# Two banks for the tail's products, and the state added to its update on TensorE

## The chip, the cores and the metric

The kernel runs on one core of one Trainium2 chip. The metric is the device time of one execution in microseconds (us). Three runs of the kernel before took 725.43, 725.92 and 728.48 us, so the time before is the median, 725.92 us.

The core has five engines with a queue each: TensorE (PE, whose weight loads the profile lists as PEld), VectorE (DVE), ScalarE (ACT), GpSimd (POOL) and SyncE (SP), which here only issues DMAs. An engine works through its own queue in order. TensorE reads operands from the SBUF memory and writes results into PSUM, which has eight banks of 2 KB per partition; VectorE and ScalarE take the results out.

## The reference

Two computations in a row. The first is a linear recurrence for each of 4 x 8 batch-heads, over 768 time steps, with a 40 x 40 state:

```
for t in range(S):
    y[t]  = r[t] @ state
    Sa    = state @ a[t]
    state = state * w[t] - outer(Sa, b[t]) + outer(v[t], k[t])
```

The second, called mixture in the kernel, takes x, the y of all heads side by side (320 wide):

```
h = relu(x @ w_in);  u, v = h[..., :512], h[..., 512:]
v_n = (v - mean(v)) / sqrt(var(v) + 1e-6)
v_s = w_spatial @ v_n + b_spatial      # over the 768 positions
out = (u * v_s) @ w_out
```

## The kernel before

**Phase 1, the steps.** The recurrence is cut into chunks of 64 positions. One *step* takes one chunk of two batches, that is 16 batch-heads: four to a *group* g (0 or 1), in each of two *parities* (partitions 0 to 39 and 64 to 103). There are 24 steps: 0 to 11 for batches 0 and 1, 12 to 23 for batches 2 and 3. The state goes from step to step in the SBUF tile `Mc`; in steps 11 and 23 no state is handed on. For each step and group the chain is: `c_bp` (L535, products with the state), `c_bp_out` (L545), `c_ff` (L553), `c_ff_out` (L561), `c_xx` (L571, into a PSUM bank of the pool `ps_c`, shown as `ch`), `c_xx_out` (L582: two ScalarE copies that read that bank, then two GpSimd selects, L396), `c_mp` (L603: the state's update, written over the last 40 columns of the same bank), `c_mp_out` (L616 adds the old state, L617 multiplies by the decay `scn` and writes `Mc`), `c_y` (L627) and `c_y_out` (L640, which frees the bank that the next step's `c_bp` fills). Beside it run, for later chunks, the decays' scans and multiplications on VectorE (L281 to L313), a triangular inversion on VectorE (L345 to L362), and small products into the pool `ps_k` (shown as `bk`).

**The mixture's products.** For a block of 128 positions of two batches (12 blocks, j = 0 to 11) there are six products in the order u, u, v, u, u, v: `m_u` (L739, 8 matmuls of 256 columns, taken out by ScalarE at L741 and stored to DRAM as `uts`) and `m_v` (L694, 8 matmuls of 512 columns, taken out at L696, normalised, and stored as `vns`). That makes 72 products, k = 0 to 71. All write the one bank of the pool `ps_m` (tile name `pv`), so a product can start only when the one before has been taken out. Before a block's products, its inputs are loaded (`m_load`, one buffer) and split in two parts (`m_split`, two buffers). All products read the weights `wh`, `wl`.

**Phase 2.** For each batch b, `vload(b)` loads `vns` (L149) and `uts` (L158, into the tile `ut0` or `ut1`), `spatial` forms 18 matmuls (L173 to L175, tile `pg`) for each of 4 x 2 results, adds the bias (L177), multiplies by u (L178, needs `ut`) and splits; `proj` forms 12 matmuls for each of three results (L193, tile `po`). In the SBUF layout of the kernel before, `ut1`, the tile of batches 1 and 3, begins at byte 153,984 of a partition and is 12,288 long; `wh` begins at byte 156,128. So `ut1` can be loaded only when the last product has read `wh`.

**Order.** Phase 1's instructions stand in a plan with due times in steps, written by hand (`at(t, ...)`), and everything due before step 24 is issued in that order, on every engine. The products are due in slots, four to a step from step 11 on; 52 of the 72 (k = 0 to 51) are due before step 24. What is due later (the *tail*: products k = 52 to 71 with what belongs to them) is issued outside the part ordered by hand, together with phase 2. There the framework's planner sets each engine's order: earlier program text has precedence, but what its own model of the chip holds not to be ready (operand, buffer) is passed over, and later text fills the place. Phase 2's text stands behind the tail's.

**PSUM.** The pools hold, in the order in which they are opened: `ps_k` banks 0 and 1, `ps_c` 2 and 3, `ps_i` 4 (`itmp`, scratch of the inversion), `ps_b` 5 and 6, `ps_m` 7. Phase 2 uses banks 0 to 3 for `pg` and 4 to 6 for `po`.

Of the kernel before, what the change touches and what calls it, by code (L numbers as in the profile page):

```python
# [8 lines left out]
F32 = mybir.dt.float32  # L9
# [5 lines left out]
ALU = mybir.AluOpType  # L15
PSUM = bass.MemoryType.PSUM
DRAM = bass.MemoryType.DRAM

P = 128
C = 64  # L20
HB = 32
E = 40
NP = 4
NB = 2
# [7 lines left out]
DH = 512  # L32

@with_exitstack
def tile_kernel(ctx, tc, early, late, vtok, win, wspT, bsp, wout, out):
    nc = tc.nc
    dram = ctx.enter_context(tc.tile_pool(name="dram", bufs=1, space=DRAM))
    B = out.shape[0]
    S = out.shape[1]
    xs = dram.tile([B, 2, NP, E, S], F32, name="xs")  # L40
    vns = dram.tile([B, S // P, P, DH], F32, name="vns")
    uts = dram.tile([B // NB, S // P, DH // P, P, NB, P], F32, name="uts")
    with ExitStack() as c1:
        phase1(c1, tc, early, late, vtok, win, xs, vns, uts, dram)
    with ExitStack() as c2:
        phase2(c2, tc, vns, uts, wspT, bsp, wout, out)
# [165 lines left out]
def phase1(ctx, tc, early, late, vtok, win, xs, vns, uts, dscr):  # L212
    nc = tc.nc
    NS = early.shape[1]
    CPB = 12
    LO, HI = slice(0, 64), slice(64, 128)
    PR = (LO, HI)
    RR = (slice(0, E), slice(64, 64 + E))
    LV = slice(0, 64 + E)

    def pool(name, bufs=1, **kw):
        return ctx.enter_context(tc.tile_pool(name=name, bufs=bufs, **kw))
# [10 lines left out]
    moe = pool("moe")  # L233
    ps_k = pool("ps_k", 2, space=PSUM)
    ps_c = pool("ps_c", 2, space=PSUM)
    ps_i = pool("ps_i", 1, space=PSUM)
    ps_b = pool("ps_b", 1, space=PSUM)
    ps_m = pool("ps_m", 1, space=PSUM)

    warm = const.tile([P, 1], F32, name="warm")  # L240
# [10 lines left out]
    ident = const.tile([P, P], F32, name="ident")  # L251
    maskp = const.tile([P, C], F32, name="maskp")
    maskn = const.tile([P, C], F32, name="maskn")
    Mc = const.tile([P, NU, C], F32, name="Mc")
# [6 lines left out]
    st = {}  # L261
# [32 lines left out]
    def scr_store(s):  # L294
        if s % CPB == 0:
            return
        sv = st["raw", s][2]
        sc = jit.tile([P, NU], F32, name="sc")
        nc.scalar.activation(sc, sv[:, :, 1], AF.Copy)
        for par in range(2):  # L300
            nc.sync.dma_start(out=scr[s, par], in_=sc[RR[par]])
# [214 lines left out]
    def grp(g):  # L516
        return slice(g * NP, (g + 1) * NP), range(g * NP, (g + 1) * NP)

    def scn_load(s):
        if s % CPB == CPB - 1:  # L520
            return
        scn = jit.tile([P, E, NU], F32, name="scn", bufs=1)
        for par in range(2):
            nc.sync.dma_start(
                out=scn[PR[par]], in_=scr[s + 1:s + 2, par].broadcast_to([64, E, NU]),
            )
        st["scn"] = scn
# [67 lines left out]
    def c_mp(s, g):  # L595
        if s % CPB == CPB - 1:
            return
        gp, ns = grp(g)
        At, Rt, tk, xf = st["blk", s]
        mp = st["xx", g][:, :, C:]  # L600
        for q, n in enumerate(ns):
            for par in range(2):
                nc.tensor.matmul(  # L603
                    mp[RR[par], q, :], lhsT=Rt[par][:, n, C:], rhs=tk[:, n, par, :],
                    start=True, stop=True,
                )

    def c_mp_out(s, g):
        gp, ns = grp(g)
        if s % CPB == CPB - 1:  # L610
            if s < NS - 1:
                nc.vector.memset(Mc[:, gp, 0:E], 0.0)
            return
        mp = st["xx", g][:, :, C:]
        mn = jit.tile([P, NP, E], F32, name="mn")
        nc.vector.tensor_tensor(out=mn[LV], in0=mp[LV], in1=Mc[LV, gp, 0:E], op=ALU.add)  # L616
        nc.vector.tensor_tensor(  # L617
            out=Mc[LV, gp, 0:E], in0=mn[LV], in1=st["scn"][LV, :, gp].rearrange("p e n -> p n e"), op=ALU.mult
        )

    def c_y(s, g):
        gp, ns = grp(g)
# [9 lines left out]
    def c_y_out(s, g):  # L632
        gp, ns = grp(g)
        c = s % CPB
        Ev = st["pre", s][0].rearrange("p (n c) -> p n c", c=WSEG)
# [8 lines left out]
    def y_store(s, g):  # L644
        c = s % CPB
        if c % 2 == 0:
            return
        b = (s // CPB) * NB + g
        t0 = (c - 1) * C
        for par in range(2):  # L650
            nc.sync.dma_start(
                out=xs[b, par, :, :, t0:t0 + 2 * C].rearrange("n e t -> e n t"),
                in_=st["y", g][RR[par]],
            )
# [28 lines left out]
        split_lo(LO_ENG, xh[64:, 2], xt[64:, 2], xh[64:, 2])  # L683
        st["xhl", key] = (xh, xl)

    def m_v(g, bq, i):
        xh, xl = st["xhl", (bq, i)]
        pv = ps_m.tile([P, DH], F32, name="pv")
        vc = slice(DH, 2 * DH)
        mm = [(xh[:, k, g, :], wh[:, k, vc]) for k in range(3)]  # L690
        mm += [(xh[:, k, g, :], wl[:, k, vc]) for k in range(3)]
        mm += [(xl[:, k, g, :], wh[:, k, vc]) for k in range(2)]
        for j, (l, r) in enumerate(mm):
            nc.tensor.matmul(pv, lhsT=l, rhs=r, start=(j == 0), stop=(j == len(mm) - 1))  # L694
        vr = st["act"].tile([P, DH], F32, name="vr", bufs=2)
        nc.scalar.activation(vr, pv, AF.Relu)  # L696
        st["vr", g] = vr
# [30 lines left out]
        nc.scalar.activation(vr, vr, AF.Identity, bias=q[:, 2:3], scale=q[:, 1:2])  # L728
        nc.sync.dma_start(out=vns[bq * NB + g, i], in_=vr)

    def m_u(d, bq, i):
        xh, xl = st["xhl", (bq, i)]
        dc = slice(d * P, (d + 1) * P)
        pu = ps_m.tile([P, NB, P], F32, name="pv")
        mm = [(wh[:, k, dc], xh[:, k]) for k in range(3)]
        mm += [(wh[:, k, dc], xl[:, k]) for k in range(2)]
        mm += [(wl[:, k, dc], xh[:, k]) for k in range(3)]
        for j, (l, r) in enumerate(mm):
            nc.tensor.matmul(pu, lhsT=l, rhs=r, start=(j == 0), stop=(j == len(mm) - 1))  # L739
        ur = st["act"].tile([P, NB, P], F32, name="ur", bufs=2)  # L740
        nc.scalar.activation(ur, pu, AF.Relu)  # L741
        nc.sync.dma_start(out=uts[bq, i, d], in_=ur)
# [4 lines left out]
    def at(t, fn, *args):  # L747
        plan.append((t, len(plan), fn, args))
# [4 lines left out]
    v, p = nc.vector, nc.gpsimd  # L753
# [10 lines left out]
    for s in range(NS):  # L764
        at(s + 0.02, scn_load, s)
        for g in range(NB):
            at(s + 0.00 + 0.05 * g, c_bp, s, g)
            at(s + 0.04 + 0.05 * g, c_bp_out, s, g)
            at(s + 0.30 + 0.05 * g, c_ff, s, g)
            at(s + 0.34 + 0.05 * g, c_ff_out, s, g)  # L770
            at(s + 0.55 + 0.05 * g, c_xx, s, g)
            at(s + 0.60 + 0.05 * g, c_xx_out, s, g)
            at(s + 0.74 + 0.02 * g, c_mp, s, g)
            at(s + 0.755 + 0.02 * g, c_mp_out, s, g)
            at(s + 0.86 + 0.04 * g, c_y, s, g)
            at(s + 0.90 + 0.04 * g, c_y_out, s, g)
            at(s + 0.95 + 0.01 * g, y_store, s, g)
# [24 lines left out]
    for q in range(GS, NS):  # L802
        t = PREP.get(q, q - 8 + 0.01)
# [20 lines left out]
            at(T_DEC + i + k * 0.12 - (0.9 if k == 0 else 0), step, gen)  # L824
    at(T_DEC + 5.9, open_act)
    slots = [T_MOE + k // 4 + (M1, M2, M3, M4)[k % 4] for k in range(3 * NS)]
    for j in range(NS // 2):
        bq, i = j // 6, j % 6
        own = slots[6 * j:6 * j + 6]
        at(max(own[0] - 1.6, 2 * j + 2.1, T_DEC + 5.92), m_load, bq, i)  # L830
        at(max(own[0] - 0.7, 2 * j + 2.7), m_split, bq, i)
        for t, d in zip((own[0], own[1], own[3], own[4]), range(DH // P)):
            at(t, m_u, d, bq, i)
        for t, g in zip((own[2], own[5]), range(NB)):
            at(t, m_v, g, bq, i)
            at(t + 0.14, m_n1, g)
            at(t + 0.42, m_root, g)
            at(t + 0.48, m_n2, g)
            at(t + 0.76, m_n3, g, bq, i)
# [12 lines left out]
    with tc.manual_schedule():  # L852
# [6 lines left out]
        for q in range(P // HB):  # L859
            rows = slice(q * HB, (q + 1) * HB)  # L860
            p.affine_select(
                out=maskl[rows], in_=maskl[rows], pattern=[[1, HB]], base=0,
# [10 lines left out]
        for m, val in ((maskp, 1.0), (maskn, -1.0)):  # L873
            p.memset(m, val)
            for rows in PR:
                p.affine_select(
                    out=m[rows], in_=m[rows], pattern=[[1, C]], base=0,
# [51 lines left out]
        n = 0  # L929
        while plan[n][0] < NS:  # L930
            t, _, fn, args = plan[n]
# [59 lines left out]
```

## Time and profile before

| what | value |
|---|---|
| runs, median | 725.92 us (725.43 to 728.48) |
| the profiled execution's own time | 728.03 us |
| its span, first to last instruction | 726.2 us |
| mean granted TensorE clock | 0.901 of full |
| PE busy | 592.8 us, 82% |
| DVE busy | 448.6 us, 62% |
| ACT busy | 415.1 us, 57% |
| POOL busy | 289.7 us, 40% |
| step 0 starts (first L535) | 29.8 us |
| step 12 starts | 305.3 us |
| step 23 starts | 524.9 us |
| last product ends | 624.1 us |

How to read what follows: times are us from the first instruction. In a table of stretches each row is one stretch with its length, then each engine's busy time (and its instructions in brackets), then the granted clock of TensorE, the DMA engines' busy share and GB/s. In a row of groups, `x22 | 6.9, 315 | 7.5 <-PE ch L603 7.5` says 22 instructions, 6.9 us busy, 315 ns each, and 7.5 us in which the engine was idle just before them, ended by line 603's matmuls. In rows of the timeline the first number is the start, the second the time to the last one's end, and a bracket holds the idle time before and what ended it. A row of the chain of waits is start, length, and what the time went to; "issue" is time for which the profile shows no wait. An fp32 matmul of the program stands as two instructions in the profile.

### The profile page before, as it was taken

Reading aid. Unit: us, or ns where it says so; the run is one execution under the profiler, and the core shown is the slowest. Engines: PE = TensorE matmul, PEld = TensorE weight load, DVE = VectorE, ACT = ScalarE, POOL = GpSimd, SP = SyncE. Lnnn points to the kernel's source line nnn. Section 1 sums busy time; section 2 is a strip of 40 time slices with the busy share of each in tenths; the row PEclk is TensorE's granted clock in tenths of the full one; section 3 lists DMA queues with packets and bytes.
Section 4 is the critical chain, followed back from the end, with each engine's and each line's share of the span. In section 5 each row is a group of like instructions: output and inputs, shape, how many; then the busy total and the mean of one; then the engine's idle time right before and its main releaser. Section 6 shows DMA issues by size and latency. Waiting matters only on the chain. (4 is left out here: it accounts for less than half of the span.)

```text
span 726.2 us, 25447 instructions
## 1 busy us (share of the span) xinstructions
PE 592.8 (82%) x10784; PEld 535.0 (74%) x10784; DVE 448.6 (62%) x884; ACT 415.1 (57%) x904; POOL 289.7 (40%) x486
## 2 busy tenths in 40 slices
PE   2707776587776877989988999899999999599997
PEld 1606665586665776868877788788789998499997
DVE  7898689968999998758797565311247201343221
ACT  2406763377655666878878798798754423332112
POOL 4102230124433435354554543464549822373221
PEclk9956997578977888989999999999899999799999
DMA  9443675294444535454365344344263533650001
GB/s 186 86 90 69 104 145 112 51 185 94 106 91 101 112 82 118 112 126 112 102 187 165 85 133 127 106 120 116 73 198 108 158 108 100 189 180 34 28 28 55
DMA packets 101337, 81.35 MB, mean 112 GB/s; under 512 B 33576, under 2 KB 90152, under 8 KB 99304
## 3 DMA queue, kind: packets, MB, share of 16 engines
q1 hardware_dynamic: 100680, 78.01, 43.3%
q10 hardware_dynamic: 544, 1.72, 1.1%
q8 instruction: 85, 1.39, 0.9%
q14 instruction: 28, 0.23, 0.1%
HBM read 59.20 MB, written 20.50 MB: 110 GB/s over the span
## 5 line engine op out<-in xcount | busy, mean ns | idle before, releaser
L396 POOL TENSOR_SCALAR_AFFINE_SELECT Rt<-Rt 64x512 f32<-64x512 f32 (+1 forms) x144 | 84.1, 585 | 102.2 <-ACT Rt L582 74.4
L545 ACT ACTIVATE Rt<-bp 64x416 f32<-64x416 f32 x96 | 49.1, 512 | 68.2 <-PE bp L535 66.4
L351 DVE TENSOR_TENSOR itmp<-A 128x30 f32<-128x30 f32 (+9 forms) x180 | 73.7, 409 | 3.3
L396 POOL TENSOR_SCALAR_AFFINE_SELECT At<-At 64x512 f32<-64x512 f32 x48 | 36.9, 768 | 94.6 <-ACT At L406 92.5
L173 PE MATMUL pg<-wsh,vh 128*128 128x384 f32 x192 | 65.1, 339 | 0.0
L174 PE MATMUL pg<-wsl,vh 128*128 128x384 f32 x192 | 65.0, 339 | 0.0
L175 PE MATMUL pg<-wsh,vl 128*128 128x384 f32 x192 | 64.8, 337 | 0.0
L355 DVE TENSOR_TENSOR A<-A,itmp 128x30 f32<-128x30 f32 (+9 forms) x180 | 59.0, 328 | 6.2
L535 PE MATMUL bp<-lin,Mc 40*64 40x104 f32 x768 | 53.1, 301 | 11.1 <-DVE y L640 10.3
L535 PEld LDWEIGHTS bp<-lin,Mc 40*64 40x64 f32 x768 | 46.2, 167 | 16.0 <-DVE y L640 13.4
L177 DVE TENSOR_TENSOR g<-pg,bb 128x384 f32<-128x384 f32 x32 | 17.7, 553 | 63.9 <-PE pg L175 56.9
L702 DVE BATCH_NORM_STATS2 bs<-vr 128x6 f32<-128x512 f32 x24 | 16.6, 690 | 60.3 <-ACT vr L696 60.2
L54 POOL TENSOR_TENSOR gl<-g,gh 128x384 fp32r<-128x384 f32 x32 | 33.8, 1062 | 47.7 <-ACT gh L50 47.7
L582 ACT ACTIVATE Rt<-ch 64x416 f32<-64x416 f32 x96 | 49.2, 512 | 3.9 <-PE ch L571 1.5
L326 PE MATMUL bk<-at,sl 64*32 64x32 f32 x1536 | 24.4, 221 | 28.6 <-DVE sl L313 14.5
L553 PE MATMUL ch<-Rt,At 128*64 128x104 f32 x768 | 46.0, 277 | 1.2 <-issue 1.2
L50 ACT ACTIVATE gh<-g 128x384 fp32r<-128x384 f32 x32 | 16.7, 522 | 52.3 <-DVE g L178 52.3
L441 PE MATMUL bk<-ident,sl 128*128 128x128 f32 x192 | 31.7, 297 | 17.4 <-ACT tk L447 6.9
L553 PEld LDWEIGHTS ch<-Rt,At 128*64 128x64 f32 x768 | 40.3, 152 | 5.7 <-issue 3.0
L326 PEld LDWEIGHTS bk<-at,sl 64*32 64x32 f32 x1536 | 20.6, 132 | 30.7 <-DVE sl L313 14.6
L571 PE MATMUL ch<-ffs,xf 64*64 64x104 f32 x768 | 42.6, 263 | 0.0
L54 POOL TENSOR_TENSOR vl<-raw,vh 128x512 fp32r<-128x512 f32 x24 | 32.1, 1350 | 25.8 <-ACT vh L50 24.8
(121 smaller groups left out, 1604.2 us busy)
## 6 DMA issues: line engine op xcount, KB each, us to landing
ein<-in_early SPq DMA_DIRECT2D x40, 387.0 KB
lin<-in_late SPq DMA_DIRECT2D x48, 160.0 KB
uts<-ur SPq DMA_DIRECT2D x48, 128.0 KB
vns<-vr SPq DMA_DIRECT2D x24, 256.0 KB
raw<-vns SPq DMA_DIRECT2D x24, 256.0 KB
ut<-uts SPq DMA_DIRECT2D x24, 256.0 KB
Rt<-in_vtok SPq DMA_DIRECT2D x48, 80.0 KB
xs<-y SPq DMA_DIRECT2D x48, 80.0 KB
```

The lines of the kernel that those rows point to most:

```text
L54: eng.tensor_tensor(out=lo, in0=x, in1=hi.bitcast(F32), op=ALU.subtract)
L173: nc.tensor.matmul(pg, lhsT=vh[:, dc], rhs=w_h, start=(i == 0), stop=False)
L174: nc.tensor.matmul(pg, lhsT=vh[:, dc], rhs=w_l, start=False, stop=False)
L175: nc.tensor.matmul(pg, lhsT=vl[:, dc], rhs=w_h, start=False, stop=(i == NT - 1))
L326: nc.tensor.matmul(pl[o:o + HB, n, :], lhsT=sl[PR[par], n, par, cs], rhs=at[PR[par], n, cs], start=True, stop=True,)
L351: nc.vector.tensor_tensor(out=tp, in0=A[:, k + 1:, k:k + 1].broadcast_to([P, m, k]), in1=A[:, k:k + 1, 0:k].broadcast_to([P, m, k]), op=AL ...
L355: nc.vector.tensor_tensor(out=A[:, k + 1:, 0:k], in0=A[:, k + 1:, 0:k], in1=tp, op=ALU.add)
L396: nc.gpsimd.affine_select(out=t, in_=t, pattern=[[0, k], [1, C]], base=0, channel_multiplier=-1, compare_op=ALU.is_gt, fill=0.0,)
L535: nc.tensor.matmul(bp[PR[par], q, :], lhsT=Mc[RR[par], n, :], rhs=li[RR[par], n, C:], start=(q == 0), stop=False, skip_group_check=True,)
L545: nc.scalar.activation(Rt[par][PR[par], gp, :], st["bp", g][PR[par]], AF.Copy)
L553: nc.tensor.matmul(ff[PR[1 - par], q, :], lhsT=At[par][:, n, :], rhs=Rt[par][:, n, :], start=True, stop=True,)
L582: nc.scalar.activation(Rt[par][PR[par], gp], xx[PR[1 - par]], AF.Copy, scale=-1.0)
```

## The change

Three edits. First, `m_u` and `m_v` get a number k, and take the bank of `ps_i` instead of `ps_m` when it is odd. k is the product's slot number where the product is due at step 24 or later, and 0 otherwise; so products due in the tail alternate between two banks, and the others use `ps_m` as before. Second, the pool `ps_b` is opened ahead of `ps_i`: `ps_b` then lies in banks 4 and 5 and `ps_i` in bank 6. Third, in steps 0 to 11 (in effect 0 to 10, since step 11 hands no state on) `c_mp` first issues, for each group, eight matmuls of the identity with the old state into the place of the update, and the update's own matmuls add to them; the VectorE addition (L616) is left out in these steps, and the multiplication by the decay reads PSUM.

```diff
@@ phase1
+    ADD_PE = range(12)
...
+    ps_b = pool("ps_b", 1, space=PSUM)
     ps_i = pool("ps_i", 1, space=PSUM)
-    ps_b = pool("ps_b", 1, space=PSUM)
     ps_m = pool("ps_m", 1, space=PSUM)
@@ c_mp
+        add = s in ADD_PE
+        if add:
+            for q, n in enumerate(ns):
+                for par in range(2):
+                    nc.tensor.matmul(
+                        mp[RR[par], q, :], lhsT=ident[RR[par], RR[par]], rhs=Mc[RR[par], n, 0:E],
+                        start=(q == 0), stop=False, skip_group_check=True,
+                    )
         for q, n in enumerate(ns):
             for par in range(2):
                 nc.tensor.matmul(
                     mp[RR[par], q, :], lhsT=Rt[par][:, n, C:], rhs=tk[:, n, par, :],
-                    start=True, stop=True,
+                    start=not add, stop=True, skip_group_check=add,
                 )
@@ c_mp_out
+        sc = st["scn"][LV, :, gp].rearrange("p e n -> p n e")
+        if s in ADD_PE:
+            nc.vector.tensor_tensor(out=Mc[LV, gp, 0:E], in0=mp[LV], in1=sc, op=ALU.mult)
+            return
         mn = jit.tile([P, NP, E], F32, name="mn")
         nc.vector.tensor_tensor(out=mn[LV], in0=mp[LV], in1=Mc[LV, gp, 0:E], op=ALU.add)
...
+    def m_ps(k):
+        return ps_i.tile([P, DH], F32, name="itmp") if k % 2 else ps_m.tile([P, DH], F32, name="pv")
+
-    def m_v(g, bq, i):
+    def m_v(g, bq, i, k=0):
...
-        pv = ps_m.tile([P, DH], F32, name="pv")
+        pv = m_ps(k)
...
-    def m_u(d, bq, i):
+    def m_u(d, bq, i, k=0):
...
-        pu = ps_m.tile([P, NB, P], F32, name="pv")
+        pu = m_ps(k)[:, 0:NB * P].rearrange("p (g t) -> p g t", g=NB)
...
+    def tail(t):
+        return slots.index(t) if t >= NS else 0
+
...
-            at(t, m_u, d, bq, i)
+            at(t, m_u, d, bq, i, tail(t))
...
-            at(t, m_v, g, bq, i)
+            at(t, m_v, g, bq, i, tail(t))
```

More of the change, by code (lines that the diff above doesn't have):

```diff
@@ L614, in c_mp_out @@
         mp = st["xx", g][:, :, C:]
+        sc = st["scn"][LV, :, gp].rearrange("p e n -> p n e")
+        if s in ADD_PE:
+            nc.vector.tensor_tensor(out=Mc[LV, gp, 0:E], in0=mp[LV], in1=sc, op=ALU.mult)
+            return
         mn = jit.tile([P, NP, E], F32, name="mn")
         nc.vector.tensor_tensor(out=mn[LV], in0=mp[LV], in1=Mc[LV, gp, 0:E], op=ALU.add)
-        nc.vector.tensor_tensor(
-            out=Mc[LV, gp, 0:E], in0=mn[LV], in1=st["scn"][LV, :, gp].rearrange("p e n -> p n e"), op=ALU.mult
-        )
+        nc.vector.tensor_tensor(out=Mc[LV, gp, 0:E], in0=mn[LV], in1=sc, op=ALU.mult)
     def c_y(s, g):
```

## The prediction

> **What bounds the kernel now.** I read the page first, then busy time by stretch, then the chain of waits and the timeline at the places that these pointed to.
>
> Its rows of busy tenths show VectorE near full in the first third and TensorE in the last, so the change's two halves lie in stages with different limits. Two stretches of the steps (step 4; steps 5 to 9):
>
> ```profile
> core 0: us, PE busy (x) PEld busy (x) DVE busy (x) ACT busy (x) POOL busy (x), PEclk, DMA share, GB/s
> 143.88:165.29 21.41, 17.98 (x489) 16.20 (x489) 13.82 (x30) 13.42 (x29) 5.04 (x8) 0.74 0.79 162
> 165.29:266.37 101.08, 74.67 (x1962) 67.03 (x1961) 98.57 (x182) 65.26 (x145) 43.53 (x50) 0.82 0.45 99
> ```
>
> In steps 5 to 9 VectorE works 98.57 of 101.08 us and TensorE 74.67: what leaves VectorE there shortens the step. In step 4 VectorE works 13.82 of 21.41 us and TensorE 17.98; there the chain through TensorE sets the end.
>
> The tail, same columns: the last six products; the time to the next matmul; what follows; the rest.
>
> ```profile
> 609.68:624.10 14.42, 10.95 (x56) 8.05 (x55) 2.08 (x6) 4.54 (x10) 3.57 (x15) 1.00 0.27 89
> 624.10:631.28 7.18, 0.00 (x0) 0.00 (x1) 2.07 (x5) 2.19 (x5) 1.39 (x7) 0.69 0.95 262
> 631.28:637.10 5.82, 5.82 (x21) 5.82 (x22) 3.78 (x5) 1.99 (x4) 4.96 (x5) 0.50 0.59 191
> 637.10:722.10 85.00, 84.96 (x521) 84.70 (x519) 23.91 (x40) 21.09 (x44) 29.52 (x27) 1.00 0.19 62
> ```
>
> From 637 on TensorE never stops, so time that it loses before is lost at the end. It loses 3.47 us in the first row (14.42 less 10.95), 7.18 us in the second, and in the third it runs at half the clock: 5.82 us of work at 0.50 is 2.91 us lost. Sum: 13.56 us. The timeline and the chain of waits say why:
>
> ```profile
> 612.23 0.63 PE L739 MATMUL pv<-xh,wh 128*128 128x256 f32 x3 [0.69 <-ACT vr L696]
> ...
> 621.98 0.97 PE L694 MATMUL pv<-wh,xh 128*128 128x512 f32 x3 [0.52 <-ACT ur L741]
> 631.28 0.63 PE L193 MATMUL po<-woh,gh 128*128 128x320 f32 x1 [7.18 <-ACT gh L50]
> ```
>
> ```profile
> 623.73 0.37 SPq L158
> 625.31 4.72 DMA ut<-uts
> 630.11 0.57 DVE g L178
> ```
>
> Each of the last six products (first and last shown) waits 0.52 or 0.69 us until ScalarE has emptied the one bank. After the last, SP issues the loads of `ut1` (it lies on `wh`, which that product reads), VectorE waits for them at L178, and TensorE for the result. Before 609.68 other work covered such waits, and ran out:
>
> ```profile
> L173 PE MATMUL pg<-wsh,vh 128*128 128x384 f32 x84 | 28.5, 340 | 0.0
> L193 PE MATMUL po<-woh,gh 128*128 128x320 f32 x24 | 7.4, 309 | 0.0
> L739 PE MATMUL pv<-xh,wh 128*128 128x256 f32 x36 | 6.7, 294 | 0.4 <-ACT vr L696 0.4
> ```
>
> These groups are of 525.5 to 609.68. L173 to L175 take turns, so 3 x 84 = 252 matmuls of `spatial`: batch 0's 144, and 108 of batch 1, four results in PSUM and two in the buffers of g, where all of them wait for `ut1`. With 3 x 24 = 72 of `proj` that is all the filler there is. L739's idle time over twelve u products (3 of these matmuls each) is 0.4 us: while filler lasted, the one bank cost TensorE almost nothing.
>
> **Part 1, the tail's second bank.** No instruction is added. What changes is when a product may start, and so where the planner puts it. Before, it put some 22 fillers between two products; the real bank was free long before. The tail's first product, then a stretch further on:
>
> ```profile
> 545.77 0.61 PE L739 MATMUL pv<-xh,wh 128*128 128x256 f32 x3
> ...
> 561.54 0.28 PE L739 MATMUL pv<-xh,wh 128*128 128x256 f32 x1
> ...
> 562.75 0.39 ACT L741 ACTIVATE ur<-pv 128x256 f32<-128x256 f32 x1 [1.40 <-PE pv L739]
> ...
> 566.31 0.86 PE L694 MATMUL pv<-wh,xh 128*128 128x512 f32 x3
> ```
>
> The bank was empty at 563.14 and the next product began at 566.31: the planner had reckoned with a slower release. With two banks two products can follow each other, and only the third waits for a release. If the distance from a product's end to the next use of its bank stays 22 fillers, a pair takes about as much time as one product did: some 5 us (566.31 less 561.54, 4.8 us; each second pair's extra v product adds a microsecond). Twenty products from 545.77 then end near 545.8 + 10 x 5.3 = 599, not at 624. `ut1` needs the 7.18 us of before, so L178 can go on near 606, and the filler (the same work, TensorE never idle) lasts to 624.1 - 3.47 = 620.6. There is room of 14 us: even products that end at 613 would leave no hole. Then the waits, the hole and its slow clock all go: 13.56 us.
>
> Lower bound: the planner leaves the last six products behind the filler, and only the 3.47 us go (less than nothing only by late operands, a rival below). Upper: 13.56. I take 12.6, near the upper end, because the room is larger than the hole; the 1.0 us off is for two stalls like the 0.4 us above. What is late next: nothing in this stage but TensorE itself.
>
> The reordered pools cost nothing while `po` manages with two banks: its third is now the products' second, free only after the last odd product. A result takes 12 matmuls, 5.29 / 3 = 1.8 us, and is emptied in 434 ns, so two are enough; a wait there would hold `proj`'s next result alone.
>
> ```profile
> 658.16 5.29 PE po L193 x36
> L194 ACT ACTIVATE ot<-po 128x320 f32<-128x320 f32 x24 | 10.4, 434 | 18.9 <-PE po L193 18.8
> ```
>
> [...]
>
> **Part 2, the state added on TensorE.** Rows of L616 and L617 over 29 to 290 us (steps 0 to 10), then of L616 in steps 5 to 9; then four rows of step 7:
>
> ```profile
> L616 DVE TENSOR_TENSOR mn<-ch,Mc 104x160 f32<-104x160 f32 x22 | 6.9, 315 | 7.5 <-PE ch L603 7.5
> L617 DVE TENSOR_TENSOR Mc<-mn,scn 104x160 f32<-104x160 f32 x22 | 11.3, 511 | 0.8
> L616 DVE TENSOR_TENSOR mn<-ch,Mc 104x160 f32<-104x160 f32 x10 | 3.1, 311 | 0.0
> 218.65 0.51 PE L603 MATMUL ch<-tk,Rt 128*40 128x40 f32 x16 [0.49 <-ACT Rt L582]
> 223.27 1.08 PE L627 MATMUL bp<-Rt,tk 128*40 128x64 f32 x16
> 224.25 0.27 DVE L616 TENSOR_TENSOR mn<-ch,Mc 104x160 f32<-104x160 f32 x1
> 226.90 0.42 DVE L640 TENSOR_TENSOR y<-bp,Et 104x256 f32<-104x256 f32 x1
> ```
>
> Removed: 22 additions of 315 ns, 6.9 us or 0.63 us a step. Added: in each of 11 steps 2 groups x 8 fp32 matmuls, two instructions each, 32 with their weight loads. Their shape (40 x 40, 40 columns) is not in the trace; the nearest rows are
>
> ```profile
> 280.39 0.95 PE L603 MATMUL ch<-tk,Rt 128*40 128x40 f32 x32
> 279.31 1.15 PE L419 MATMUL bk<-lin 40*64 40x64 f32 x32
> ```
>
> Less the last one's 0.21 us, L603 takes one every 24 ns and L419 (40 rows too, 64 columns) 30 ns: 0.77 to 0.96 us a step, 8.4 to 10.6 us in all. I take 0.77, since 40 columns is L603's case. They wait for the same ScalarE copies (L582) as L603, since they overwrite what these read; the wait only moves ahead, and what is queued behind it on TensorE (L603, L627, the next step's L535) is late by 0.77 us.
>
> Where VectorE is the limit, that is covered: in step 7 L603 ends at 219.16 and L616 begins at 224.25; L627 ends at 224.35 and the last L640 begins at 226.90. In steps 2, 3 and 5 to 9 L616 never waits (idle 0.0 in 5 to 9; the 7.5 us of its waits lie in steps 0, 1 and 4), so 7 x 0.63 = 4.4 us are gained. In steps 0, 1, 4 and 10 VectorE waits for TensorE at L616 or L640: 0.77 more against 0.63 less, 4 x 0.14 = 0.6 us lost. Net 3.8 us; bounds: 6.9 if VectorE sets all eleven, and 8.4 us lost if TensorE does. Were VectorE's cover gone, a step would lose the 0.77 us.
>
> L617 then reads PSUM instead of SBUF. The nearest pair reads 384 columns, L177 from PSUM and L178 (its form's row) from SBUF:
>
> ```profile
> L177 DVE TENSOR_TENSOR g<-pg,bb 128x384 f32<-128x384 f32 x32 | 17.7, 553 | 63.9 <-PE pg L175 56.9 <-POOL gl L54 7.1
> L178 DVE TENSOR_TENSOR g<-g,ut x32: 544/558/1639, 547.4 to 712.2; 128x384 f32<-128x384 f32 x32
> ```
>
> 553 against a median of 558 ns: no charge. [...]
>
> **Sum.** 12.6 + 3.8 = 16.4 us off the profiled execution's 728.03 (span 726.2 and 1.8 around it) is 711.6. The median of the runs lies 2.1 us under that execution, so 709.5.
>
> **Rivals.**
>
> *The order of the tail stays* and only the six waits go, 3.5 us: 725.9 - 3.5 - 3.8 = 718.6. For it: the planner's reckoning isn't the chip's, and I infer its spacing. Against: the last block's split comes at 586.36 (below), and filler lasted 23 us longer.
>
> *TensorE sets the steps.* Part 2 loses up to 8.4 us instead of gaining; half of that, 4.2, with part 1 whole: 717.5. For it: step 4's row. Against: steps 5 to 9's.
>
> *Slower: products reach TensorE's queue ahead of their operands.* TensorE works in order, so a product placed earlier that waits for its split inputs or an eviction holds up all filler behind it. ScalarE, in order too, once stands still for 4.74 us behind a load, and the last block's split and a product's eviction stand behind it:
>
> ```profile
> 585.83 0.63 ACT L50 ACTIVATE vh<-raw 128x512 fp32r<-128x512 f32 x1 [4.74 <-DMA raw<-vns]
> 586.36 0.83 ACT L50 ACTIVATE xh<-xt 128x768 fp32r<-128x768 f32 x1
> 587.10 0.58 ACT L696 ACTIVATE vr<-pv 128x512 f32<-128x512 f32 x1
> ```
>
> If five of the tail's ten pairs met such a wait in full, 23.7 us against 16.4 gained, the time would be 725.9 + 7.3 = 733.2; it decides from 16.4 us of such stalls. Against: the tail's order had 0.4 us of them in 84, with this one in it.
>
> *It does not do what it says:* the planner uses the second bank but spaces products as before, the hole stays, and only part 2 counts: 722.1.
>
> **How the numbers follow.** Forecast 0.58 (709.5; its own range 705 to 714), tail's order stays 0.17, TensorE sets the steps 0.10, no effect in the tail 0.08, late operands 0.07. The range 703 to 720 reaches from all bounds at their best (725.9 - 13.6 - 6.9 = 705.4, and 2 us for the spread of runs) past the first two rivals. A change of 0.5% (3.6 us) is about what can be told from none: faster 0.83, same 0.10 (the fourth rival and a little of the second), slower 0.07.
>
> **What would show it.** Right: no idle TensorE over 1 us between 600 and 640, `ut1`'s loads issued some 15 us ahead of the filler's end, steps 5 to 9 shorter by 0.6 us each, L616 only from step 12. Wrong: a gap before a `po` matmul with a clock of 0.50 after it; L617 or L640 waiting for TensorE in steps 5 to 9; products idle on xh.

## The result, and the profile after

The changed kernel takes 707.31 us (705.49 to 711.40) against 725.67 (725.31 to 728.48): ratio 0.9728, 95% interval 0.9694 to 0.9763, 18.4 us less. A second series beside other kernels gave 706.63 against 725.97: ratio 0.9753 (0.9709 to 0.9797). Forecast were 709.5 us and a range of 703 to 720. The profiled execution is the slowest of its four: 711.40 us, span 709.5.

The tail first: busy time by stretch of the changed kernel, with the columns of the prediction's rows. The stretches are step 22, then 544.70 us to the end of the last product, and what follows up to 640 us:

```profile
503.00:522.81 19.81, 19.60 (x368) 16.49 (x368) 4.28 (x11) 16.71 (x38) 11.07 (x24) 1.00 0.33 96
...
544.70:598.63 53.93, 52.13 (x311) 48.97 (x310) 21.64 (x42) 24.88 (x51) 41.29 (x74) 1.00 0.48 145
598.63:640.00 41.37, 41.27 (x255) 40.95 (x254) 13.65 (x23) 14.37 (x32) 20.75 (x24) 1.00 0.57 179
```

Its timeline at the two waits that are left, at the last product, and at the loads of `ut1` and the first use of them:

```profile
583.42 0.63 PE L753 MATMUL pv<-xh,wh 128*128 128x256 f32 x3 [1.00 <-ACT ur L755]
...
586.12 0.62 PE L753 MATMUL itmp<-xh,wh 128*128 128x256 f32 x3 [0.78 <-ACT vr L710]
...
598.01 0.62 PE L708 MATMUL itmp<-wh,xl 128*128 128x512 f32 x2
601.30 5.38 SPq L158 DMA_DIRECT2D ut<-uts  x7
...
607.70 1.03 DVE L178 TENSOR_TENSOR g<-g,ut 128x384 f32<-128x384 f32 x2 [3.20 <-DMA ut<-uts]
```

The last product ends at 598.63 instead of 624.10, `ut1`'s loads are issued from 601.30 on, L178 goes on at 607.70, and TensorE works 41.27 of the 41.37 us from the last product to 640, at full clock. Neither the hole nor the half clock behind it is left. From the start of step 23 (the stretch of 201.25 us quoted below) the kernel takes 709.5 - 522.81 = 186.7 us, 14.6 less; step 22 takes 19.81 instead of 22.19, 2.4 less.

The steps. Steps 5 to 9 of the changed kernel, the same columns:

```profile
167.67:268.43 100.76, 79.89 (x2127) 71.86 (x2120) 96.35 (x175) 65.48 (x145) 43.97 (x50) 0.82 0.46 101
```

Groups of 29 to 290 us: the identity matmuls and the state's multiplication out of PSUM; then VectorE's waits in steps 5 to 9, where the kernel before had one, of 1.6 us at the row of L337:

```profile
L606 PE MATMUL ch<-Mc,ident 40*40 40x40 f32 x352 | 11.6, 210 | 4.0 <-issue 3.8
L626 DVE TENSOR_TENSOR Mc<-ch,scn 104x160 f32<-104x160 f32 x22 | 9.0, 435 | 10.8 <-PE ch L612 7.1 <-ACT Rt L430 2.8 <-ACT Rt L583 0.9
```

```profile
DVE Lc L338 <- PE bk L327: 1.3, 3, 0.6
DVE y L651 <- PE bp L638: 1.0, 1, 1.0
```

VectorE has 96.35 us of work in steps 5 to 9 instead of 98.57, and the steps take 100.76 instead of 101.08: in this execution the state's half bought next to nothing there. VectorE's wait for y (L651) is one of the signs that the prediction named for being wrong. So the gain lies where it was forecast, but the tail gave more than the bound of 13.56 us, and the state less than its 3.8. The experiments take these two apart.

### The profile page after: what moved, and what is told of

Its sections match the earlier page's. It is cut to its first block, busy times and chain, and to the rows that moved or that the text cites. A ratio compares the mean times of both kernels' runs of the same rounds, so it can differ in the third digit from the quotient of the medians.

```text
span 709.5 us, 26133 instructions
## 1 busy us (share of the span) xinstructions
PE 593.6 (84%) x11136; PEld 538.4 (76%) x11136; DVE 437.5 (62%) x862; ACT 414.7 (58%) x904; POOL 290.3 (41%) x486
## 5 line engine op out<-in xcount | busy, mean ns | idle before, releaser
L352 DVE TENSOR_TENSOR itmp<-A 128x30 f32<-128x30 f32 (+9 forms) x180 | 75.3, 419 | 3.2
L536 PE MATMUL bp<-lin,Mc 40*64 40x104 f32 x768 | 53.5, 302 | 15.4 <-DVE y L651 11.7
L536 PEld LDWEIGHTS bp<-lin,Mc 40*64 40x64 f32 x768 | 46.7, 168 | 18.3 <-DVE y L651 13.7
L554 PE MATMUL ch<-Rt,At 128*64 128x104 f32 x768 | 47.5, 283 | 0.0
L554 PEld LDWEIGHTS ch<-Rt,At 128*64 128x64 f32 x768 | 42.1, 158 | 4.5 <-issue 1.9
L716 DVE BATCH_NORM_STATS2 bs<-vr 128x6 f32<-128x512 f32 x24 | 16.6, 691 | 41.6 <-ACT vr L710 41.5
L638 PE MATMUL bp<-Rt,tk 128*40 128x64 f32 x768 | 32.5, 240 | 10.1 <-issue 10.1
L572 PEld LDWEIGHTS ch<-ffs,xf 64*64 64x64 f32 x768 | 38.3, 143 | 1.4 <-ACT Rt L583 0.2
```

The lines of the kernel that those rows point to most:

```text
L352: nc.vector.tensor_tensor(out=tp, in0=A[:, k + 1:, k:k + 1].broadcast_to([P, m, k]), in1=A[:, k:k + 1, 0:k].broadcast_to([P, m, k]), op=AL ...
L536: nc.tensor.matmul(bp[PR[par], q, :], lhsT=Mc[RR[par], n, :], rhs=li[RR[par], n, C:], start=(q == 0), stop=False, skip_group_check=True,)
L554: nc.tensor.matmul(ff[PR[1 - par], q, :], lhsT=At[par][:, n, :], rhs=Rt[par][:, n, :], start=True, stop=True,)
L572: nc.tensor.matmul(xx[ev, q, :], lhsT=xf[ev, n, :], rhs=ffs[ev, q, :], start=True, stop=True,)
```

## Experiments

Beside whole times, lengths of stages are used, since the early steps scatter from run to run (the last section has the stops behind it): one kernel measured twice (the wide identity, below) gave ratios of 0.9733 and 0.9826, while steps 14, 17, 18, 20 and 21 have the same length in every profile here to within some 0.1 us. A step runs from its first L535 matmul (L536 after the change) to the next step's. A *stop* is a time in which TensorE stands still in the middle of its work; for most stops of the early steps the profile shows nothing that TensorE waits for. A *pair* is one weight load and its matmul in the profile.

### Each half alone, and the whole again

Tail alone: 

```diff
-    ADD_PE = range(12)
+    ADD_PE = range(0)
```

> The second bank in the tail alone; the state is added on VectorE in all steps, as before. By the prediction part 1 is worth 12.6 us (bounds 3.5 and 13.56), so about 713 against 725.7, ratio 0.983. The profiled run of the changed kernel took 14.6 us less from step 23 on (186.7 against 201.25 us); if that is part 1 and the state part gives nothing, 711 and the same time as the changed kernel. If the state part is worth its predicted 3.8 us, this kernel is 3.8 us slower than the changed one; if the state part loses the 2.65 us by which step 12 began later in that profile, this one is 2.65 us faster.

Measured: 707.80 us, ratio 0.9758 (0.9713 to 0.9803). State alone:

```diff
     def tail(t):
-        return slots.index(t) if t >= NS else 0
+        return 0
```

(and `ps_i` ahead of `ps_b` again).

> The state added on TensorE in steps 0 to 11 alone; all products in one bank, PSUM pools in the old order. By the prediction -3.8 us: 721.9, ratio 0.995. By the profile of the changed kernel (step 12 began 2.65 us later than before): 725 to 728, ratio 1.000 to 1.004, with VectorE waiting for TensorE at the state's multiplication and at y. The rival that TensorE sets all steps: up to +8.4 us, 734.

Measured: 724.95 us, ratio 0.9987 (0.9950 to 1.0023). The whole again, on the same chip:

> The changed kernel again, beside the others on the same chip, in more rounds: 705.5 to 711.4, ratio 0.97 to 0.98. If places where TensorE stands still with nothing shown to wait for decide the step times, the start of step 12 moves by some 2 us from run to run; if the order of the work does, it stays within 0.5 us of the first profile's 307.99.

Measured: 706.63 us, ratio 0.9753 (0.9709 to 0.9797); step 12 began at 304.25, not at 307.99.

The tail alone is worth 18.2 us with an interval of 14.3 to 20.8; the state alone 1.0 us (3.6 less to 1.7 more); the whole is 1.2 us faster than the tail alone, which the scatter of the runs does not tell from nothing. The forecast of 12.6 lies below the tail's interval, that of 3.8 for the state just outside its own.

What the forecast of the tail missed is in step 22. The kernel before: the step in two parts, what follows it, then its timeline at the point between the parts:

```profile
502.76:517.85 15.09, 13.49 (x273) 11.87 (x273) 2.49 (x7) 13.91 (x32) 7.14 (x13) 0.99 0.32 88
517.85:524.95 7.10, 7.07 (x89) 5.47 (x89) 1.78 (x4) 3.21 (x8) 4.49 (x13) 0.54 0.27 80
524.95:726.20 201.25, 186.01 (x1184) 177.66 (x1184) 62.53 (x114) 64.49 (x134) 86.62 (x131) 0.97 0.34 107
```

```profile
516.28 0.51 PE L603 MATMUL ch<-tk,Rt 128*40 128x40 f32 x16 [0.40 <-ACT Rt L582]
517.85 0.77 PE L603 MATMUL ch<-tk,Rt 128*40 128x40 f32 x16 [1.07 <-ACT Rt L582]
```

And the kernel with the tail alone: step 22, what follows it, and its timeline at the same place:

```profile
501.44:521.25 19.81, 19.59 (x369) 16.50 (x369) 4.21 (x11) 16.71 (x38) 11.02 (x25) 1.00 0.33 96
521.25:707.60 186.35, 180.43 (x1176) 173.53 (x1176) 60.12 (x114) 64.17 (x135) 87.11 (x132) 1.00 0.37 116
```

```profile
512.71 0.63 PE L708 MATMUL itmp<-wh,xh 128*128 128x512 f32 x2
...
514.97 0.51 PE L612 MATMUL ch<-tk,Rt 128*40 128x40 f32 x16
515.40 0.50 PE L708 MATMUL itmp<-wh,xh 128*128 128x512 f32 x1
...
516.97 0.51 PE L612 MATMUL ch<-tk,Rt 128*40 128x40 f32 x16
```

The planner takes the first product of the second bank (k = 53, at 550.71 us in the kernel before) and puts it, in two pieces, just where TensorE stood waiting for ScalarE's copies (L582). Before, that stop took 1.07 us, and behind it TensorE ran at a mean clock of 0.54 to the step's end. What TensorE lost from step 22 on, before: 1.60 us idle and 7.07 x 0.46 = 3.25 us by the clock in step 22, then 0.45 + 3.47 + 7.18 idle, and 2.91 by the clock behind the hole, 18.9 us. After the change: 0.21 + 1.80 + 0.10 = 2.1 us idle up to 640, none by the clock. The difference, 16.8 us, is near what the whole stretch shows: 223.44 us before, 206.50 after, 16.9 less. The size depends on the execution. The kernel with the state alone has the same stop in step 22, followed by less time at half clock, and takes 21.18 us for that step and 224.37 from its start on; the second profile of the changed kernel takes 205.65 from there on, 18.7 less. The time won in step 22 appears partly behind it, since the product that fills the stop is no longer there.

### What of the second bank closes the hole

Two kernels with the state on VectorE. In one, only the very last product (number 71) uses the second bank; in the other, the first ten of the tail's twenty:

```diff
-        return slots.index(t) if t >= NS else 0
+        return slots.index(t) if slots.index(t) == 71 else 0
```

> Only the tail's very last product uses the second bank; state on VectorE. In TensorE's order 72 filler matmuls (some 23 us) then stand behind the last product and ahead of the first one that needs ut1, against none before and 117 in the changed kernel. Theory that the tail's gain is the hole: it closes although 19 of 20 products still share a bank; 7.18 us and the 2.91 us of half clock behind it go, most of the six waits for ScalarE and the stop in step 22 stay: -10.1 us, 716, ratio 0.986. Rival that every alternating product saves its share (17.3 us over 20 products): -0.9 us, 725.

```diff
-        return slots.index(t) if t >= NS else 0
+        return slots.index(t) if t >= NS and slots.index(t) < 62 else 0
```

> The tail's first ten products alternate, the last ten share one bank; state on VectorE. TensorE's order then has no filler between the last product and the first matmul that needs ut1, as before. Theory: the hole of some 7 us and its slow clock stay; what goes is the stop in step 22 (2.4 us in the profile of the kernel with the tail alone, by a product that fills it) and some 3 of the 3.47 us of waits: -5.4 us, 720.5, ratio 0.9926. Rival that every alternating product saves its share: -8.6 us, 717.

Measured: one product 721.88 us, ratio 0.9946 (0.9908 to 0.9984); ten products 720.32, ratio 0.9900 (0.9824 to 0.9975). By stage (step 22; the rest), the kernel with one product, with its waits from 504 to 640 us:

```profile
504.73:525.96 21.23, 19.29 (x360) 16.22 (x360) 4.11 (x11) 17.09 (x39) 11.61 (x25) 0.92 0.31 89
525.96:719.80 193.84, 183.74 (x1184) 175.25 (x1184) 61.13 (x114) 63.88 (x134) 86.96 (x131) 1.00 0.36 111
```

```profile
PE pv L708 <- ACT ur L755: 2.3, 2, 1.8
PE pv L753 <- ACT vr L710: 2.1, 3, 0.7
PE pv L753 <- ACT ur L755: 1.6, 3, 0.5
```

and the kernel with ten, with its timeline behind the last product:

```profile
502.27:522.07 19.80, 19.59 (x369) 16.50 (x369) 4.22 (x11) 16.70 (x38) 11.02 (x24) 1.00 0.34 96
522.07:718.90 196.83, 182.29 (x1176) 175.39 (x1176) 60.95 (x114) 65.04 (x135) 87.60 (x132) 0.98 0.35 110
```

```profile
616.58 5.18 SPq L158 DMA_DIRECT2D ut<-uts  x7
...
624.75 0.64 PE L193 MATMUL po<-woh,gh 128*128 128x320 f32 x1 [7.79 <-ACT gh L50]
```

One alternating product suffices to close the hole: no wait for `gh` is left, and step 23 on takes 7.4 us less. It is not the expected 10.1, because the waits for ScalarE rose to 6.0 us from 3.92 (0.45 + 3.47): eight products in a row now wait without filler instead of six. Ten alternating products fill the stop in step 22 (19.80 us again) and leave 2.6 us of waits for ScalarE out of 3.92, but the hole stays, 7.79 us long; from step 22 on this kernel takes 6.8 us less than before. So the two large terms belong to two different products, the first and the last. An equal share for each of twenty products (16.9 / 20) would have been 0.8 us for the one product, not 8.4. For the ten it would have been 8.5, which lies near the 6.8, but the hole that is still there speaks against it. In step 22 the two kernels are compared with a profile whose clock stayed low for long: the one-product kernel has the stop too, takes 21.23 us instead of 22.19, and so owes 1.0 of its 8.4 us to the clock and not to its product. The one-product kernel's whole time gained 3.9 us only by its ratio, less than its 8.4 from step 22 on; its profile reached step 22 2.0 us later than before, with the same order of work up to there, and the rest of that difference isn't explained.

### What the state's half costs and brings

First, one half exaggerated at a time. The identity matmuls issued three times:

```diff
-            for q, n in enumerate(ns):
-                for par in range(2):
+            for rep in range(3):
+                for q, n in enumerate(ns):
...
```

> As the changed kernel, with each step's identity matmuls issued three times into the same place (the first two are overwritten; same result): 1.54 us more TensorE work in each of 11 steps than in the changed kernel. If VectorE covers it, as predicted, in the seven steps 2, 3, 5 to 9, only the four others get longer: +6 us, 713. If TensorE sets all steps: +17 us, 724. If nothing but the stops without a shown wait count: 707.

Measured: 720.08 us, ratio 0.9926 (0.9888 to 0.9965). And the tail alone with VectorE's addition issued four times:

```diff
-        nc.vector.tensor_tensor(out=mn[LV], in0=mp[LV], in1=Mc[LV, gp, 0:E], op=ALU.add)
+        for rep in range(4 if s < 12 else 1):
+            nc.vector.tensor_tensor(out=mn[LV], in0=mp[LV], in1=Mc[LV, gp, 0:E], op=ALU.add)
```

> The second bank in the tail, the state added on VectorE and the addition issued four times in steps 0 to 10 (same result): 1.89 us more VectorE work in each of 11 steps than in the kernel with the tail alone (707.8). If VectorE sets seven steps, as predicted: +13.2 us, 721. If it sets all eleven: +20.8 us, 729. If TensorE sets them: 708 to 711.

Measured: 722.38 us, ratio 0.9987 (0.9954 to 1.0020). Steps 5 to 9 of the two, each in its own profile:

```profile
173.31:278.03 104.72, 83.27 (x2448) 75.50 (x2441) 96.46 (x175) 65.39 (x145) 43.38 (x50) 0.86 0.43 98
```

```profile
165.73:277.57 111.84, 75.17 (x1962) 67.56 (x1961) 108.30 (x212) 65.09 (x145) 44.79 (x50) 0.82 0.41 90
```

Without the state part these five steps take 101.20 us in the mean of five profiles (100.77 to 101.57), with it 99.53 in the mean of three (100.76, 99.27, 98.55). VectorE's 5 x 1.89 = 9.5 us more lengthened them by 10.6: VectorE does set these steps. But TensorE's 5 x 1.54 = 7.7 us more lengthened them by 5.2, where full cover would have been nothing. Of these 5.2 us step 8 has 2.9 (23.72 against 20.8): TensorE stood still within the update's products, with nothing shown to wait for, and VectorE waited for them:

```profile
252.96 0.63 PE L613 MATMUL ch<-tk,Rt 128*40 128x40 f32 x12 [3.46 <-issue]
253.73 0.43 DVE L627 TENSOR_TENSOR Mc<-ch,scn 104x160 f32<-104x160 f32 x1 [4.48 <-PE ch L613]
```

The whole kernels: with VectorE's addition fourfold 14.6 us more than the tail alone, where 13.2 were expected if VectorE sets seven steps; with the identities threefold some 13 us more than the changed kernel, between the expected 6 with cover and 17 without. Of these 13 us step 0 has 4.9 (46.88 us against 42.0 in the mean of three).

Then each part by itself. No addition on either engine in steps 0 to 10; the identity matmuls and VectorE's addition both (the matmuls' result is overwritten, `start=True` on the products); and 49 more identity matmuls in step 0 alone, for the place of instructions (the first and the third with `ADD_PE = range(0)`):

```diff
+        if s < 11:
+            nc.vector.tensor_tensor(out=Mc[LV, gp, 0:E], in0=mp[LV], in1=sc, op=ALU.mult)
+            return
         mn = jit.tile([P, NP, E], F32, name="mn")
```

> Second bank in the tail; in steps 0 to 10 the old state is neither added on VectorE nor on TensorE (that part of the computation is left out, the state is only the step's update times its decay). VectorE has 0.63 us a step less than in the kernel with the tail alone (707.8), TensorE's instructions are the same ones at the same places. If VectorE sets steps 5 to 9 down to that size, they take 101.2 - 3.2 = 98.0 us (101.2 is the mean of the four profiles without the state part) and the whole 4.4 us less, 703.4. If something else sets them as soon as VectorE has less, they stay above 100 and the whole within 1 us of 707.8.

```diff
-                    start=not add, stop=True, skip_group_check=add,
+                    start=True, stop=True, skip_group_check=add,
...
-        if s in ADD_PE:
-            nc.vector.tensor_tensor(out=Mc[LV, gp, 0:E], in0=mp[LV], in1=sc, op=ALU.mult)
-            return
```

> As the changed kernel with its identity matmuls, but their result is overwritten and the addition stays on VectorE (same result): TensorE's work and program of the changed kernel, VectorE's of before. If VectorE's addition is what counts in seven steps, as predicted: 4.4 us more than the changed kernel (711), 0.6 us more than the kernel with the tail alone. If TensorE's 0.77 us a step counts as well: up to 716. Steps 5 to 9 (99.5 us in the mean of three profiles with the state part, 101.2 without): 102.7 by the first, 101.2 or less if only the place of the stops counts.

```diff
+        if s == 0:
+            for rep in range(24 + g % 2):
+                nc.tensor.matmul(
+                    mp[RR[0], 0, :], lhsT=ident[RR[0], RR[0]], rhs=Mc[RR[0], ns[0], 0:E], start=True, stop=True,
+                )
```

> The kernel with the tail alone and 49 identity matmuls of 40 columns more in step 0, overwritten at once: 98 pairs of weight load and matmul, which puts every later TensorE instruction 98 pairs further on in its program, as the 352 pairs of the state part do from step 11 on if TensorE stops at every 127th pair (352 less 2 x 127 is 98). Theory that the stops without a shown wait belong to places in the program: steps 12, 13 and 15 take the lengths that they have with the state part (20.0, 20.3, 21.6 us in the mean of three profiles) and not those without it (23.3, 19.4, 20.6 in the mean of four). Rival that the state part itself shortens step 12: 23.3, 19.4, 20.6 stay. Time: 707.8 - 3.3 + 0.9 + 1.0 and some 2.4 us for the 49 matmuls in step 0, 709.

Measured: without any addition 705.69 us, 2.1 less than the tail alone, ratio 0.9712 (0.9658 to 0.9766); both 711.35, ratio 0.9799 (0.9756 to 0.9841); 49 more in step 0 713.87, ratio 0.9833 (0.9788 to 0.9878). Steps 5 to 9 without any addition, then with both:

```profile
165.89:263.30 97.41, 72.49 (x1961) 64.82 (x1960) 94.64 (x172) 65.38 (x145) 44.46 (x50) 0.87 0.46 102
```

```profile
170.35:272.57 102.22, 77.00 (x2129) 69.11 (x2121) 99.06 (x184) 65.39 (x145) 43.72 (x50) 0.85 0.45 98
```

These steps took the lengths that were expected if VectorE sets them (98.0 and 102.7); the whole without any addition lies between its two expectations, 703.4 and some 707.8, and the whole with both at its lower one, 711. The four corners of steps 5 to 9: VectorE's addition alone 101.20, neither 97.41, identities alone (the change) 99.53, both 102.22. Taking the addition away saves 3.8 us without the identities and 2.7 with them, 3.2 in the mean, and 5 x 0.63 = 3.15 was forecast. Putting the identities in costs 2.1 without the addition and 1.0 with it, where nothing was forecast. The change keeps 1.7 of the 3.2. Two of the corners are single profiles, and the three of the change differ by 2.2 us, so these costs are rough. VectorE's idle time in the five steps (their length less its busy time) is steadier: 2.5 to 2.8 us in the five profiles with the addition alone, 2.77 with neither, 4.41, 4.14 and 3.16 with the identities, 3.16 with both. By it the identities make VectorE wait 1.1 us more without the addition and 0.6 more with it, in the mean; what is left of the 2.1 and 1.0 is VectorE's own work between the marks, which also scatters (95.13 to 96.35 us in the three profiles of the change).

The third kernel tests where steps change length. Step 12 of the kernel before, of the changed kernel, and of the one with 49 more matmuls in step 0:

```profile
305.34:329.19 23.85, 20.41 (x465) 18.02 (x457) 14.40 (x34) 17.13 (x41) 11.33 (x18) 0.87 0.56 121
```

```profile
307.99:328.32 20.33, 18.26 (x465) 16.02 (x456) 13.98 (x33) 16.39 (x39) 10.94 (x17) 1.00 0.65 140
```

```profile
310.23:330.65 20.42, 18.30 (x465) 16.07 (x457) 13.97 (x33) 16.45 (x40) 11.04 (x17) 1.00 0.67 141
```

The changed kernel's step 12 is 3.5 us shorter, and the same happens with no state on TensorE when the program is only shifted by 98 pairs. So this gain is a matter of the place at which TensorE stops, and of the clock behind the stop (0.87 against 1.00), not of the state. All fourteen profiles agree: step 12 takes 22.8 to 24.3 us in the six kernels whose TensorE program has nothing added ahead of it, and 19.7 to 20.8 in the eight with anything from 88 to 1056 pairs more. Step 13 followed too (20.21, expected 20.3), step 15 did not (20.74, expected 21.6). The whole of that kernel was 5 us over its expected 709: step 0 took 50.52 us instead of 41.5, though step 1 took 17.23 instead of some 21.8; why step 0 grew by more than the 2.4 us of matmuls stays open.

### One wide identity

Instead of four identity matmuls of 40 columns, one of 160:

```diff
-            for q, n in enumerate(ns):
-                for par in range(2):
-                    nc.tensor.matmul(
-                        mp[RR[par], q, :], lhsT=ident[RR[par], RR[par]], rhs=Mc[RR[par], n, 0:E],
-                        start=(q == 0), stop=False, skip_group_check=True,
-                    )
+            for par in range(2):
+                nc.tensor.matmul(
+                    mp[RR[par]], lhsT=ident[RR[par], RR[par]], rhs=Mc[RR[par], gp, 0:E],
+                    start=True, stop=False, skip_group_check=True,
+                )
```

> As the changed kernel, but the old state enters PSUM by one identity matmul of 160 columns for each parity and group instead of four of 40: 4 instead of 16 matmuls in a step, 44 instead of 176 pairs of weight load and matmul in all, times two passes. If TensorE's extra instructions eat the gain on VectorE (0.77 us a step against 0.63), most of it comes back: about 0.4 us a step on TensorE, 2 to 4 us less than the changed kernel, some 704. If the cover by VectorE holds as predicted, nothing changes: 707 to 709.

> The changed kernel with one identity matmul of 160 columns for each parity and group once more, to see whether its first profile was chance: there steps 5 to 9 took 97.26 us, as in the kernel without any addition (97.41), against 99.53 in the mean of three profiles with four identities of 40 columns. If the 352 narrow pairs cost the difference, 97.0 to 98.0 again, and the whole 2 us less than the changed kernel, ratio 0.971 against its 0.973 and 0.975. If the first profile was chance: 99 to 101, ratio 0.974.

Measured: 705.86 us, ratio 0.9733 (0.9683 to 0.9782), and then 712.12, ratio 0.9826 (0.9773 to 0.9880). Steps 5 to 9 of the first and of the second:

```profile
160.40:257.66 97.26, 72.47 (x2007) 63.33 (x2000) 94.95 (x172) 65.27 (x145) 44.53 (x50) 0.89 0.47 104
```

```profile
168.51:265.70 97.19, 77.86 (x2008) 68.66 (x2000) 94.98 (x172) 65.28 (x145) 45.19 (x50) 0.83 0.47 103
```

Both times these steps take what they take without any addition, and VectorE's idle time (2.31 and 2.21 us) is no longer than there: with 88 pairs instead of 352 the identities cost nothing here. Whether the smaller number does it is not shown, because the stops move too: neither profile has one in step 8, where the four identities cost most. The whole kernel is not shown to be faster than the changed one: its two ratios differ by more than that.

## Why the prediction was right and wrong

**The hole (right, by its steps).** Products were forecast to end near 599 and ended at 598.63; L178 near 606, it was 607.70; the hole, its half clock and the short waits went, but for the two stalls for which 1.0 us had been taken off (1.78). The one-product kernel shows the hole's cause by itself. That the tail's order changes, against the rival of 718.6, was right, and no product was seen waiting for its split inputs, the rival of late operands.

**The tail's size (too small, and the bound wrong).** The step that failed is the one that put the loss "From 637 on TensorE never stops, so time that it loses before is lost at the end" into the stretch from 609.68 on and named its 13.56 us the upper end. The first alternating product belongs to step 22, where the kernel before lost 1.60 us idle and 3.25 by the clock. The term should have been 16.9 us (223.44 - 206.50; 18.7 in the later pair of profiles), not 12.6. Step 22's row was there to be read; the prediction began at the tail's first product at 545.77, while the planner brought the second one (k = 53) forward by some 36 us, into step 22.

**The state's gain on VectorE (right).** 3.15 us were forecast in steps 5 to 9, the two pairs of kernels give 3.8 and 2.7. L617's reading from PSUM was to cost nothing; its row even got shorter, from 511 to 435 ns, 0.8 us in ten of them. With the 3.15 that makes 3.9, and VectorE's work in these steps fell by 3.9 with neither addition (98.57 to 94.64).

**The identities' cost (wrong).** L603 was the right model for their size: L606 has 352 matmuls of 210 ns where L612, the update's products, has 352 of 213. The step that failed is "Where VectorE is the limit, that is covered". In steps 5 to 9 the identities cost 1.0 to 2.1 us by length and 0.6 to 1.1 by VectorE's waits. Nearly all of these waits have one place: in step 8 VectorE is idle 1.89, 2.23 and 1.22 us in the profiles of the identities alone and 0.93 with both, against 0.76 with neither and 0.43 before. Step 8 takes 20.8 us in the mean of four profiles with 16 identities a step (the change twice, the state alone, and both additions), 19.8 in the mean of six without them. The timeline of the changed kernel there, TensorE and then VectorE, against the kernel before:

```profile
246.65 0.61 PE L638 MATMUL bp<-Rt,tk 128*40 128x64 f32 x13 [3.24 <-issue]
...
247.30 0.42 DVE L651 TENSOR_TENSOR y<-bp,Et 104x256 f32<-104x256 f32 x1 [1.03 <-PE bp L638]
```

```profile
245.61 0.86 PE L326 MATMUL bk<-at,sl 64*32 64x32 f32 x45 [2.36 <-issue]
```

TensorE stops for 3.24 us with nothing shown to wait for, within the matmuls that y needs, and VectorE waits for it. In the kernel before, the stop of that step fell into L326, and VectorE had no wait for y in steps 5 to 9. So what failed is less the size of the cover than its place: the added matmuls moved the stop into products that VectorE needs. That is argued from these rows; no run moved the stop in step 8 alone. The cover of 5.09 and 2.55 us read from step 7 held in step 7 (20.0 us in the mean of the three profiles with the state part, 20.6 without) and was taken for all of them. Outside steps 5 to 9 no gain or loss of the state part can be told from the scatter.

**The sum.** 16.4 us were forecast, 18.4 and 19.3 measured; the tail's term was some 4.3 us too small, the state's nearly 3 too large. That the forecast of 709.5 came within 2.2 us of the measured 707.31 is in part luck, since the two errors have opposite signs. The range did not need that luck: with either error alone the forecast would have been 705.2 or 712.3, and its lower end had taken both bounds at their best.

## What to carry to other kernels

When a resource is doubled for some operations, look at every stretch from which the planner may now draw them forward, and count the stops there as part of the possible gain; an operation is worth most where it fills a stop. One product moved at the tail's end (7.4 us from step 23 on) was worth more than ten at its start (6.8 from step 22 on). And a "hidden" cost of many small instructions should be checked in every step, not in one: here narrow identity matmuls, 32 pairs a step, cost up to 2.1 us in five steps, most of it in one of them, where 8 wide pairs a step cost nothing measurable.

## What was not expected of the hardware

**TensorE's stops lay 127 pairs apart in its program, or a multiple of that.** The profile puts down to "issue" the waits of TensorE for nothing that it shows. Those of the kernel before in 29 to 290 us:

```profile
PE bk L326 <- issue: 12.4, 6, 3.2
...
PE ch L603 <- issue: 3.0, 3, 1.2
PE bk L389 <- issue: 2.7, 1, 2.7
PE bk L504 <- issue: 2.6, 1, 2.6
PE bp L627 <- issue: 2.5, 1, 2.5
...
PE bk L458 <- issue: 1.2, 1, 1.2
PE ch L553 <- issue: 1.2, 1, 1.2
```

Together 14 stops and 25.6 us; over all profiles of this study 9 to 17 such stops of more than 0.25 us, 18 to 32 us in all, up to 340 us, and behind it none to two, 1.9 us together at most. Counted in the order of the trace, those of the kernel before fall on matmuls 859, 985, 1113, 1240, 1367, 1621, 2639, 2893, 3020, ...: 127 apart, or a multiple of it, give or take two. The page's row for the queue that carries instructions, of the kernel before, the changed one and the one with the identities three times:

```profile
q8 instruction: 85, 1.39, 0.9%
```

```profile
q8 instruction: 87, 1.43, 0.9%
```

```profile
q8 instruction: 93, 1.52, 0.9%
```

These are packets of 16.4 KB (1.39 MB in 85). The three kernels have 10784, 11136 and 11840 pairs, so 352 and 1056 pairs more came with 2 and 8 packets more. What makes TensorE stand at these places is not shown: no run changed these transfers. What the runs do show: moving the program by 98 pairs moved step 12 by 3.4 us, and the same kernel's early steps differ by several us from execution to execution. In the two profiles of the changed kernel such stops sum to 22.5 and 17.7 us in 29 to 290 us, and step 12 began at 307.99 and 304.25. That is why a change that adds instructions to early steps shifts times it has nothing to do with.

**A stop of 1.07 us can be followed by half the clock.** In step 22 of the kernel before (clock 0.54 for the 7.10 us behind the stop, in the row above) and, behind the 2.62 us stop of step 12, from 323.70 to the step's end:

```profile
323.70:329.19 5.49, 5.45 (x121) 4.95 (x121) 1.44 (x5) 1.22 (x4) 0.13 (x1) 0.50 0.17 42
```

All three profiles with that stop in step 22 show the slow clock behind it: for 6.83 us in the kernel before, for some 3.4 us in the kernel with the state alone and in the one with one product in the second bank. The same stop in step 19, 1.07 us long in both, was followed by 3.41 us at half clock in the kernel before and by the full clock in the changed kernel. The six shorter waits ahead of the hole, 0.52 to 0.69 us each, kept it at 1.00 (609.68 to 624.10 in the kernel before); with 1.07 us that holds only at times. In the profiles of the kernel before and of the changed kernel every stretch at half clock but the last one begins on a grid of 3.41 us and lasts a whole number of its periods: in the kernel before, those of steps 16, 19, 22 and of the hole begin at 404.97, 459.59, 517.61 and 626.84 us, which are 16, 17 and 32 periods apart, and last 3.41, 3.41, 6.83 and 10.24 us. What decides whether a stop of 1.07 us costs the clock is not shown: no run moved a stop of one length.
